# One PSUM tile of seven banks instead of two score tiles and three others, with a new written-out order, in an attention and Fourier-filter kernel

## The chip, the core and the metric

The kernel runs on one core of one Trainium2 chip. TensorE (PE in the profile) multiplies, VectorE (DVE) and ScalarE (ACT) read its results out of PSUM, GpSimd (POOL) works on SBUF, and SyncE (SP) issues most of the transfers. Inputs come from and the output goes to device memory. The metric is the device time of one execution in microseconds (us); the kernel before took 381.3 us as the median of three runs (380.2 to 381.46).

## What is computed

The input x has 2048 tokens of 448 features. One half of the result is self-attention with 16 heads of 28 features and a full softmax over all 2048 keys, then a projection with wo. The other half is a Fourier filter over the whole 2048x448 array. A gate per token mixes the two.

```
qkv = (x @ wqkv).reshape(B, S, 3, 16, 28) ...        # q, k, v per head
p   = softmax(q . k * 28**-0.5)                       # 16 heads, 2048 x 2048 each
a   = (p . v).reshape(B, S, 448) @ wo
b   = irfft2(rfft2(x) * (w_r + 1j * w_i))             # over tokens and features
g   = sigmoid((x * gate_w).sum(-1))
out = g * a + (1 - g) * b
```

## The kernel before

**Attention.** The heads lie in four groups g of four; a head is padded to 32 rows, so that the four heads of a group fill the 128 partitions. Queries are cut in four chunks c of 512. So there are 16 outputs n = (g, c). For each of them the kernel goes through 16 key tiles kt of 128 keys, and each key tile has four units, one per head s. The score of a unit is one matmul of a 32x128 tile of k against 512 queries; matmuls of different heads sit in different row tiles of the array and run side by side (a row pass). The result fills one PSUM bank of 128x512 numbers.

A unit then goes one of two ways. In 187 key tiles ("a") ScalarE takes the exponential of two banks at a time (line 1034, 374 times, 1024 numbers per partition) into `ring`, an SBUF buffer of 28 slots, and four matmuls in four column tiles multiply it with v into the bank `pvb` (a column pass). In the other 69 key tiles ("d", list `ND`) VectorE turns a score into the bits of a bf16 power of two by one add and clamp to uint16 (line 993, 276 times, one bank each); GpSimd makes three more phases of it by an integer add (line 1003, 207 times); and all four phases go through their own column pass into `pvb`. When an output n is complete, VectorE copies `pvb` out (`normalise`, line 1166 and, for the last one, 1137), takes reciprocals, and multiplies (lines 1178 and 1159).

**The rest.** The projections of q, k and v, the Fourier transforms as matmuls with constant matrices, the product with the filter weights, and the output (`out_tile` and `last_tile`, lines 1208 and 1229: eight column passes for each 128 tokens, four of the Fourier rows `X` against `Bd`, 224 columns wide, and four with wo, 448 wide) are called background. They are put between the scores.

**PSUM.** `alloc` (line 330) shares out the eight banks: `psA` and `psB` (lines 334 and 335), two banks each, hold scores for ScalarE alone and are used in turn; `pvb` is one bank; three banks `bgt` (line 337) serve everything else, the scores of the "d" tiles included. An operation that needs one of the three has an `Item`, whose bank number is set before it is emitted.

**The order.** The operations of the whole kernel are first collected by `Sched.op`. The order in which they are emitted, and so the order on each engine, is written out in `TABLE`, a compressed list of operation numbers with a list of bank numbers; `Sched.run` (line 275) goes through it, and a number from 60000 on emits a filler, a matmul whose result nobody reads (line 681, six passes). `pin` (line 302) holds every instruction at its place in its engine's order. Nothing is chosen at run time: an engine that reaches an instruction whose data or whose bank is not ready waits there, and everything behind it on that engine waits as well. The waits themselves are worked out by the framework per tile: two instructions that touch the same PSUM tile are ordered, also where they touch different banks of it.

Of the kernel before, what the change touches and what calls it, by code (L numbers as in the profile page):

```python
# [29 lines left out]
UNITS = 128.0  # L30
# [8 lines left out]
    "eNoN1mNjWEsUQNHxnMG5SW2ltm3bNtPUtm3btm3bto3UdvveX9hf1jakJbHEkXCCJDqJQWKSWCQ2iUPikngkPiEkAUlIEpHEJAkJI0lJMpKc"  # L39
    "UJKCZCApSU6SiniSmuQijHQlQAKiCScZSRoiSXaSlkQlitQk6Ugmkp7UILVINZKNZCG5SVUSheQhWUkOUodkJiVJKRKNlCa1SV5SloSQUFKO"  # L40
    "1Cf5SH5SgBQiBUkxUp6UIRVJYVKEFCXFySZSgWwmlUgJ0oq0JVvIVrKStCPbyHayiqwmVcgOsoZMJGtJZTKJTCZTyFSyjqwnG0g3YpVXG8l0"
    "MoPMJLOIU7PJHDKX7CTziCDzySy/gCwkcWk8Gp8uIovJDL+ELCUJaEK6jKDaRRLRnqQxWU5WkECFqMQ0Ck1Co9JoNDqNQcNoTBqLxqZx6G6y"
    "h+wl+0ioak6iqqfkGXlOXpCXJILcIQ3IfhJJ7pID5B55RV6TKOo+eUMekI7kIXlEHpNo6iCJrqaRGKouOUSS0mQ0pupEYqnkNAU9TJ6Qt2SD"
    "j63ekfckjvpA4qp4qhc5Qo6SlDS+akGOkan0I/lEptHPpAlJoBKq6fQLSaS+Qip6nCRWJ0hqmkR9gxk0TH0lp8hpkoau8WnpGXKWJFX1SG9y"
    "jpwnF8hMepEkU61JOnqJXCZXyFVyjSRX18kNcpOkULfIbZKeplRlaAaakZ4kmWhinoSnUj+hLE2t0qhYvByNzcvTXxCNz/XpVFpVgX6H6Dy9"
    "oqYiHUQyqIzqG0nGm5HvJAaPyX+Qn6Qp+UUyqT+QWf2DSjSLyqo6k+okDk/OK9OGpArtSDvRuDwhX+ezqc60C82uEvD1PhEP439IUp5D/SX/"
    "CKGUMrrac9qV5lSCSqqoprkU0Kw0G81Oc9DcKif9TXLR3NRQS/PQPCovzUdTcEfzKk/z05keaUDj83wqhBagmWlBWogWpkVofpWFhtJ4vCgt"
    "RtuTNqQ47U4LqIw8E+9BS9Ke1PJCyhhtHC+oCqv0vIjiJgMvTaUppoqqtLy4siYlr0p70RKqGi2pqtNSKh0vrVJzYXrTUlSZYaSMKkHT8Bq0"
    "Jk3FmSmrsvFyipi/UF5l5dn5SFpB5eGjaEU1mlZSeXkOPobWopVVB/IbqqiqKhcfS535AdVUTg6mNq2ucvMaqh7tQurTBjQfr0NrKm9qqc+u"
    "MC/DG9J4Bk1dWlsV4XVUDNOI1FUFeEJTkNdTCUwjmpnXV1l4WV6IJzHFeQlegefnFXkDFcs0VDFNXFOTN1KNVWNandfg8U0TVZQnMk1VMhOY"  # L50
    "YryZim1K8lo8jglXIaa5qsRb08o8mklpWqgIVY6X5m1oW9qOtlItVXnenjbjrVUqE86/uaimB2mjEpsmtK1KbkJNO1WVN6XNeQQPM9X4F9de"
    "NeFNeQeV0Xx3P9xP98t1VN1oJ1WX1+MZTDjtoprT7qSz+u0iaBTzx1XhLWhX1ZK2591UJlOKd1cduPQ9lPLpTHrTU/VSrWhtXoeDN9763iqN"
    "6aNa8+imr3I+tRlMve+n0po2vL8aQtE34o35ABX4gSqFSWoym0FqKB1GB6shqi3/6xrwf244JZ76+rwdH6oa8qKG+WGqI2/FC5jhqqDpxkeo"
    "fIb7Qkb4kWqU6sU78eKmO89jSpjRKovpzceoljyr6UvGqh68Jw/xXXkLXsaE+qG8GR2n8prxqjOP7xP4YTyhH8wnqES+iBnC4/i4PrGfqPrQ"
    "SWqyym860C58iipsipmpKokP81F9NN+HT1PZTHRf2cTw09UMNVP15aVNH5LT9KWzVAqf0s9Wa30qH9PH8rF9at+PpvFlzRy1kKb1i+hiOosu"
    "oXPVUprOD+fzVDkzgvfn5c18NYYvUHfoXXqPrqD36QO6ki5UI+gq+pA+oo/pE7qarqFP6SI1lq+l6+h6uoEO4BvpM7pYae/5JjqOL1HP6Qu6"
    "mb6kkXQ8f0WXqtd0C91Kt9FBdDtdpsbT5WoCXaFWquV0IK9kNvoddBwdSEuZQTypX6WS+Yl0El2tZvI1ajKdzquZmmatGs1n8XVqvZrEa5iS"
    "pqLZoPrxyXwG36jm8lF8Np9CJ/A5fCTfpPrTWmYi36yqmwF0Hp/Ct6gKpoqparapZXyrmk13qCW8tgk3c+g0nstsV03MPLpTNTUr+HKewyzl"
    "u1Qzs1vN5xFmj1rE1/LspoVZyTfyxXw+3ac6mTw+r9+rxpCFPJ9fx/P7TfyAmkv3qwK+oG9r2pmD6pA6rPbwOqa1mcqbm728kD+idvBMfifP"
    "7LP4oyqr38wHkGPqFF1AT9Mz9Cw9R7P54+o8vUCz+xz+Ir1EL9MTajW/Qrfwq3QVv0av0xv0pKprbtJTah9fw7uaBby/6WNu0dv0jFrPT6vc"  # L60
    "Zj9vY97QKL6zOad20rNqF91N99DzagPfS/fR/fQAPUgP0QtqFz9Md/Mj9Cg9Ri+q43QZPUFP8kuqgzlJT/GO5hzfzi+ro/wYv6KuqlZmG+9h"
    "eprz/Dg/wa+pLia9v64y+BvqMK9nuptDPLk/wluam+qWus/7mduqgq/oe5mG5gG/o7byC/wir+Qr+7uqij/IQ3goz+jbmwO8kbmnBphu5r6q"
    "6h+om7yaf6j6mt7mPb3C39K7fKCpbx6pW/yxOs3P8idqmhllnqqrfDi5xO/xZ2qcGW/e0RfquXrCL/OyfqIp55/ya3y0eakiVRPfwLxSTf0Y"
    "81rd5s38ZPNGhfs7/AV/q5r7l/ydivAzTDFf3JfwJX0p38K/V/PNB9WflPaRfJB5xT+qT2q2iefL+Bv8DL/OJ5np5rP6ogabIeQRf8af88J+"
    "gvmqvqnH/Av/yhubsaaIf8inmO/qh+JMsE/8p/qlPvOpRjLFNBtK3vJ3/D3/rf6omWaO+av+8n98sVloiP7AP/J/SorlZpYhYoihWgmm+5Hh"
    "huvXfK5ZYRaZN/w3L+qFpuIPlzqnz+V/8G+8oVda6wXmO8/th5lGfpmJKn5y0L+40UvMPPM/SMLqbn6p8drpaMIK1N39SpOE9fA9fS8PLLro"
    "7QO9yYSxpGyECdGhOoZIxvr47aaxj6qFiKKTMycOmW2Gieg6mtYiVHgRQ4OIIraY3SamiCVi6h1mp6nuY+lAxNYJxFGTUMTRIWK/SSJQ1PBx"
    "dZjYZ/aYeDq+TqDjiaEmvqjla/s6vq6v51eZ1SaRSCzq+7giqWjgy/uEerOZ7deYRHqUH+3H+LE+sR7nx/sJfq+ZQE6aOT6JDtNpxFbT0ifV"
    "yXRynVa08W19O9/exxEXTAff0Y80KXRKvc7U9J38QdPKf6Cp9Ef6iaYTqXUanVwcM+nFZ5pWp9OpRGyRXp8xJ8xh84WmFhl0Rl1I7DKFRV/f"
    "z6cQ030ykUmfNwdMZp1FZ9U5RUqRS3T2XXwGsdYcN9l0PnHKZNcD/EA/yGcU+cVgP8Tn0Dl1EXHEFBWnTSaRS2cVQ/1Zk1vHYHl0NnHOxGTD"  # L70
    "fD6dV180XX1mEYtlEbFZft3f3zIFdEEdh2UXf+h685fmEHlEIb3BFNYlxT9aStwx5UURTVgFQVleUVQ/N7lFaXHJFNNTfHE91d8zZcRDU0KX"
    "1DXEffPAlNI1RWldQBQU70w8VkaXFa19OXHbxGfFxHBfVidgI3xCVk1UFIlYdVFOV9Dl9RNTQnyjE/1I/9J8pxV1FVFJ/6A/aRU9yVfWTQVj"
# [12 lines left out]
    "U9q8dp8eT1aIjWKd2Kv36/2sgH3r3/n14r3fLg7oD/6gzmQz2t3ijz+kc9jDOredJI7ojz4G7hBbRRq7XETDbSI6bhEMOR7Vm8UecUwLlKgw"
    "nx1Ljuv8NgquFCf0IZHTHhbZ7Cl9Um8Sx8RpndXmscdFIXtR7BS7xBl9Vj9iUfGcLm0vifO6rP3kjwiNKfCCvqgT2fK2kt0vjopL+ry4IB6z"
    "z/4Je8qesefssn7BEtuXDDCSXdFX9QFR1Ra2X/xX/82H4EFxTV/XBr97iw5Pin3ih7+hf3qPr9hr9oa9Ze/Ye/aZfWE3dSgmQ8QPLMymwq/s"
    "G/vObukAf7Cf7Bf7zf6wU+Iju63/sn+McMoZT2I5F1zyT0zxIlbzO7qujYmx8J6+q88Kw+/rcyI2PtA17EN9QsTBuFjLPtJl7GPd1D7RT/UN"
    "cVqcERVtftwrilrgDWxSvCmSY3X7TN8R5ewL/VxfEdfEXVHBXhUvdU1b2UbqW+K6aGar2Nvitf4oXumH4q1OauvY+PhGV7PvdD0bD9/rR+KD"
    "fixei8b2nvgkGtrc+EYUt0/EU/FMfNT17XvxSafEB2Ic+azTYFr8opvYy+K5+CC+6m/6vhhMvuu34oX4od+JdFjSNrKpsbYNt7/Eb/FTJ8CE"  # L90
    "+FtPs790HpxrE+EfnR6jyb96tk2MSbC5/Sr+6RmWQE78IiiE4UL7Sqy0GXC6jS6L2T+CwSLL4a/4JiKsAAk/BJM/RQk7x5ZHBS9FC5sLNcy0"
    "30V4JMDn/yNHCiGVLGXzopTz7SxLZT400NpaqIwgIyIjIsMjPRhZCQugg4qYCQtiIQwAYZmdZzOiliHwTxTGIhgim2KoDIVGWAwzYxRwMgtm"
    "xbU2KkSDKHK5XWC9jA4r7BYbX8aEGBBVZsPVNjvmwApYFFHGlbGgLMaTCWRsiAPlcIndbAO5waaWcWGNjQexpZVxZBOMD4ttAiAyjayCVTEh"
    "xJAJ5SqbCBLJxJBcxpRLbRKohsUxDFLINrYEtrQlcb1tjEkhqayONTCWbGWTQSlMDutsMtkQN9pNNptMIrfagSQFpISUsjtml6lgnz1sU0Mq"
    "GY5poDQ2wywyTJbBbnjUHrFpoQdmlekgvcwkM8sDNj3klRlkBsgom2MEnrTpZCbYZlvgVZtPZoQskBlq4il7yGaFlphbtsI2WEK2xmyQHY7b"
    "WnjOlpR5ZCmZA3LCdlsbc8mxWAfrYmfMBfttaTkaz9vckAfyQj28aLtgfbxh88t8kB8aYGKZVra1PfGgzSkLQEFZEE7YArKY7IqFoJDMIQvL"
# [1374 lines left out]
```

## Time and profile before

| | us |
|---|---|
| runs, median (lowest, highest) | 381.3 (380.2, 381.46) |
| span of the profiled execution | 379.2 |
| TensorE busy | 371.3 (98%) |
| VectorE busy | 339.1 (89%) |
| ScalarE busy | 351.1 (93%) |
| GpSimd busy | 234.4 (62%) |
| first and last exponential, start | 12.74 and 364.96 |

The profiled execution has a span of 379.2 us from its first to its last instruction; the timed runs were 1.0 to 2.26 us longer, the median 2.1. A row of the timeline gives the start, the duration, the engine, the line and operation, output and inputs by the program's names, and how many instructions the row holds. TensorE's matmuls are pipelined: several run side by side, and the end of one overlaps the start of the next, so that the time a pass costs is read from the distance between starts and not from the duration in the row. 32\*128 in a row is the tile of the array: 32 rows by 128 columns is a row pass, 128\*32 a column pass. TensorE's clock was granted in full throughout.

### The profile page before, as it was taken

Reading aid. Unit: us, or ns where it says so; the run is one execution under the profiler, and the core shown is the slowest. Engines: PE = TensorE matmul, PEld = TensorE weight load, DVE = VectorE, ACT = ScalarE, POOL = GpSimd, SP = SyncE. Lnnn points to the kernel's source line nnn. Section 1 sums busy time; section 2 is a strip of 40 time slices with the busy share of each in tenths; the row PEclk is TensorE's granted clock in tenths of the full one; section 3 lists DMA queues with packets and bytes.
Section 4 is the critical chain, followed back from the end, with each engine's and each line's share of the span. In section 5 each row is a group of like instructions: output and inputs, shape, how many; then the busy total and the mean of one; then the engine's idle time right before and its main releaser. Section 6 shows DMA issues by size and latency. Waiting matters only on the chain.

```text
span 379.2 us, 12643 instructions
## 1 busy us (share of the span) xinstructions
PE 371.3 (98%) x5117; PEld 142.4 (38%) x5117; DVE 339.1 (89%) x665; ACT 351.1 (93%) x389; POOL 234.4 (62%) x264
## 2 busy tenths in 40 slices
PE   8999999999999999999999999999999999999996
PEld 6634223342433333234333434233333323433564
DVE  1768899999999999999999999999999999988744
ACT  2799999999999999999999999999999999999841
POOL 4446465866778866565553565778597778483510
PEclk9999999999999999999999999999999999999999
DMA  6511101010210112211322212223222122222132
GB/s 145 157 34 44 29 18 36 4 36 2 41 52 22 44 41 54 55 38 30 68 60 93 69 40 49 57 61 70 45 64 74 30 69 72 86 64 72 35 103 75
DMA packets 31158, 21.23 MB, mean 56 GB/s; under 512 B 16260, under 2 KB 29052, under 8 KB 31100
## 3 DMA queue, kind: packets, MB, share of 16 engines
q1 hardware_dynamic: 29708, 19.96, 20.7%
q8 instruction: 40, 0.66, 0.7%
q10 hardware_dynamic: 1392, 0.46, 0.5%
q14 instruction: 18, 0.15, 0.1%
HBM read 14.51 MB, written 1.96 MB: 43 GB/s over the span
## 4 chain that ended last, share of the span: by engine, by line
PE 55%; ACT 31%; issue 6%; DVE 4%; DMA 2%; POOL 1%; SPq 0%; DVEq 0%; ACTq 0%; POOLq 0%
ACT ring L1034 31%; PE bg L432 24%; PE pvb L432 17%; PE psA L432 7%; PE psB L432 6%; DVE pd L993 2%; PE bg L435 1%; DMA CS<-cCS 1%; DVE X L1419 1%; POOL pd L1003 1%; DMA Wg<-in_B_w_i_dram 0%; DVE X L1298 0%; DVE q L1178 0%; DVE t L1362 0%; DVE wpq L1224 0%
## 5 line engine op out<-in xcount | busy, mean ns | idle before, releaser
L1003 POOL INT64_ADD pd<-pd x207 | 211.9, 1038 | 96.7 <-DVE pd L993 27.4
L1034 ACT ACTIVATE ring<-psA 128x1024 bf16<-128x1024 f32 x187 | 201.7, 1078 | 4.7 <-PE psA L432 3.2
L1034 ACT ACTIVATE ring<-psB 128x1024 bf16<-128x1024 f32 x187 | 201.7, 1079 | 2.6 <-PE psA L432 1.4
L993 DVE TENSOR_SCALAR pd<-bg 128x512 uint16<-128x512 f32 x276 | 180.9, 681 | 8.5 <-PE bg L432 3.5
L432 PE MATMUL pvb<-pd,vd 128*32 128x512 bf16 x1104 | 96.9, 384 | 0.1
L432 PE MATMUL bg<-q,k 32*128 32x512 bf16 x276 | 96.3, 383 | 0.2
L432 PEld LDWEIGHTS <-k 32*128 32x128 bf16 x1024 | 40.1, 91 | 122.4 <-issue 117.7
L432 PE MATMUL psB<-q,k 32*128 32x512 bf16 x374 | 73.2, 383 | 1.3 <-ACT ring L1034 0.7
L432 PE MATMUL psA<-q,k 32*128 32x512 bf16 x374 | 72.8, 383 | 0.5 <-ACT ring L1034 0.2
L432 PE MATMUL pvb<-ring,vw 128*32 128x512 bf16 x748 | 67.9, 384 | 0.0
L432 PEld LDWEIGHTS <-vd 128*32 128x32 bf16 x1104 | 25.3, 94 | 35.5 <-issue 31.1
L432 PEld LDWEIGHTS <-vw 128*32 128x32 bf16 x748 | 17.5, 94 | 22.7 <-issue 20.5
L432 PEld LDWEIGHTS <-xT 128*128 128x128 bf16 (+5 forms) x512 | 20.3, 97 | 10.7 <-issue 9.7
L432 PE MATMUL bg<-xT,wpq 128*32 128x512 bf16 (+3 forms) x244 | 21.2, 383 | 0.1
L1362 DVE TENSOR_TENSOR t<-bg,Wg 128x450 bf16<-128x450 f32 x32 | 18.8, 614 | 0.6 <-DMA Wg<-in_B_w_i_dram 0.4
L432 PE MATMUL bg<-xT,wpk 128*32 128x512 bf16 (+2 forms) x240 | 18.9, 383 | 0.0
L432 PE MATMUL bg<-wvr,xT 128*128 128x112 bf16 (+2 forms) x192 | 13.7, 213 | 0.0
L1178 DVE TENSOR_TENSOR q<-pvs,Rb 128x512 bf16<-128x512 f32 x15 | 10.9, 729 | 2.6 <-DMA Rb<-rsc 2.6
L1298 DVE TENSOR_TENSOR X<-bg,oc 128x226 bf16<-128x226 f32 (+1 forms) x32 | 12.3, 386 | 0.5
L432 PEld LDWEIGHTS <-CS 128*32 128x32 bf16 x384 | 9.0, 95 | 9.9 <-issue 5.6
L432 PE MATMUL bg<-xtok,CS 128*32 128x225 bf16 (+1 forms) x192 | 11.2, 294 | 0.7 <-DMA CS<-cCS 0.7
L742 DVE TENSOR_SCALAR k<-bg 128x512 bf16<-128x512 f32 x15 | 10.3, 685 | 1.3 <-PE bg L432 1.1
(117 smaller groups left out, 315.4 us busy)
## 6 DMA issues: line engine op xcount, KB each, us to landing
Rb<-rsc SPq DMA_DIRECT2D x60, 64.0 KB
CS<-cCS SPq DMA_DIRECT2D x16, 192.0 KB
V<-xtok SPq DMA_DIRECT2D x16, 113.0 KB
Wg<-in_B_w_i_dram SPq DMA_DIRECT2D x64, 28.1 KB
xtok<-Ab SPq DMA_DIRECT2D x16, 112.5 KB
xtok<-in_A_x_dram SPq DMA_DIRECT2D x3, 448.0 KB
Wg<-in_B_w_r_dram SPq DMA_DIRECT2D x32, 28.1 KB
out_dram<-wpq SPq DMA_DIRECT2D x6, 112.0 KB
```

The lines of the kernel that those rows point to most:

```text
L432: self.pin(self.nc.tensor.matmul(out, lhsT=lhsT, rhs=rhs, start=start, stop=stop, **kw))
L435: self.pin(self.nc.tensor.transpose(out=out, in_=in_, identity=self.c("ident")[0:n, 0:n]))
L742: self.pin(nc.vector.tensor_scalar(out=dst, in0=self.bgi(it), scalar1=SQ, scalar2=None, op0=ALU.mult))
L993: self.pin(nc.vector.tensor_scalar(out=ys[:, s, :].bitcast(U16), in0=self.bgi(it), scalar1=127 * UNITS, scalar2=0.0, op0=ALU.add, op1=ALU. ...
L1003: self.pin(nc.gpsimd.int64_add(out=fl(pds), in0=fl(ys), in1=PHASE[f] * 0x0001000100010001))
L1034: self.pin(nc.scalar.activation(out=self.ring[:, u0:u0 + len(st), :], in_=slot[:, 0:len(st), :], func=ACT.Exp, scale=LN2 / UNITS))
L1178: e = self.dve(dv(512), lambda: self.pin(nc.vector.tensor_tensor(out=dst, in0=pvs[:], in1=self.Rb[:], op=ALU.mult)), ds, kk, lk=True)
L1298: self.pin(nc.vector.tensor_tensor(out=free_dims(self.X1[:, t, :], [[F, 2], [-1 if dif else 1, n]], (F - 1) * dif), in0=free_dims(self.bgi ...
L1362: self.pin(nc.vector.tensor_tensor(out=out[:], in0=self.bgi(it)[:, 0:F2].rearrange("p (a f) -> p a f", a=2), in1=free_dims(Wg[:], [[F, 2], ...
L1419: self.pin(nc.vector.tensor_tensor(out=free_dims(self.zt[0:FN], [[128, 4], [1, 128]], 512 * t), in0=self.bgi(it)[0:FN, :].rearrange("p (a ...
```

## The change

`psA`, `psB` and the three banks `bgt` become one tile `ps` of seven banks; `pvb` stays. Every score unit is now an operation of its own with a bank of its own out of the seven, and so are the transposes and projections at the start and the last output tiles, which used `psA` and `psB`. An exponential reads two neighbouring banks, whichever pair they are. As all seven banks are one tile, `pin` tells the framework for each instruction which banks it uses, and that it does not depend on instructions with other banks; what an operation names as its own inputs is kept. In 12 of the 69 "d" tiles two of the four clamps are put together as one instruction over two neighbouring banks (`PARTS`), which leaves 264 clamps. Due times, which were no longer used for the order, are taken out. `TABLE` now has four lists: 4001 operation numbers, 1199 banks, the widths of the exponentials (374, all two banks) and the parts of the 69 "d" tiles. The order is another one throughout, and it has no fillers.

```diff
 TABLE = (
-    "eNoN1mNjWEsUQNHxnMG5SW2ltm3bNtPUtm3btm3bto3UdvveX9hf1jakJbHEkXCCJDqJQWKSWCQ2iUPikngk
+    "eNoNltMSIDoWAMMTJ2Pbtm3btm3btm3btm3btnFn9w/6oaurFTKoJ9KoK2qKKqGOqBlyyKOGqBtqiyxCCCOC
...
+    def need(self):
+        return [p for d in self.op_now.deps for p in d.made]
...
+    PARTS = (((0,), (1,), (2,), (3,)), ((0, 1), (2, 3)), ((0, 2), (1, 3)), ((0, 3), (1, 2)),
...
     def pin(self, ins):
...
+        if self.sc.used:
+            used = frozenset(self.sc.used)
+            keep = [p for p, u in self.sc.need() if not used & u]
+            if ins.ins.engine in self.before:
+                keep.append(self.before[ins.ins.engine])
+            for other in self.bank_sets:
+                if not used & other:
+                    self.tc.declare_no_dep(ins.ins, group="bank" + repr(sorted(other)), reason="other banks",
+                                           keep=[k for k in keep if k.name in self.bank_sets[other]])
+            self.bank_sets.setdefault(used, set()).add(ins.ins.name)
+            self.tc.add_to_no_dep_group("bank" + repr(sorted(used)), ins.ins)
...
-        self.psA = ps.tile([P, 2, 512], F32, name="psA")
-        self.psB = ps.tile([P, 2, 512], F32, name="psB")
+        self.ps = ps.tile([P, 7, 512], F32, name="ps")
         self.pv = ps.tile([P, 512], F32, name="pvb")
-        self.bgt = [ps.tile([P, 512], F32, name=f"bg{i}") for i in range(3)]
...
     def bgi(self, item, dt=F32):
-        t = self.bgt[item.bank][:]
+        t = self.ps[:, item.bank, :]
+        self.sc.used.add(item.bank)
...
+            for part in self.PARTS[sc.parts[di]]:
...
+                    self.pin(nc.vector.tensor_scalar(
+                        out=free_dims(ys[:], [[512 * e, w], [1, 512]], 512 * part[0]).bitcast(U16),
+                        in0=self.ps[:, bs[0]:bs[0] + w, :],
+                        scalar1=127 * UNITS, scalar2=0.0, op0=ALU.add, op1=ALU.max))
...
-            slot = self.psA if i % 2 == 0 else self.psB
-            deps = [exps[i - 2]] if i >= 2 else []
+            deps, ms = [], []
...
+                it = uit[n, kt, s] = Item()
...
+                m = sc.op("PE", 0.22, fm, self.kev[g, kt // 4] + self.qev[g, c], 0.0, 0.0, "row", it, name="score")
...
+                self.pin(nc.scalar.activation(out=self.ring[:, u0:u0 + len(st), :],
+                                              in_=self.ps[:, bs[0]:bs[0] + len(st), :],
+                                              func=ACT.Exp, scale=LN2 / UNITS))
...
-        it = Item() if i > 1 else None
-        bank = lambda: (self.psA[:, 0, :] if i == 0 else self.psB[:, 0, :] if i == 1 else self.bgi(it))[:, 0:D]
+        it = Item()
+        bank = lambda: self.bgi(it)[:, 0:D]
```

Three places show how instructions move. The first is TensorE in the middle of the attention, at a row pass with scores for both ways. In the rows of before, `psB` and `bg` are scores of `q` and `k`, and the engine named in brackets is the one whose reading of the bank the matmul waits for.

```order
L432 MATMUL psB<-q_85,k_89 128x512 [waits Activation_49]
L432 LDWEIGHTS k_89
L432 MATMUL psB<-q_85,k_89 128x512
L432 LDWEIGHTS k_89
L432 MATMUL bg_64<-q_85,k_89 128x512 [waits DVE_49]
```

```order
L464 MATMUL ps<-q_81,k_85 128x512 [waits Activation_49]
L464 LDWEIGHTS k_85
L464 MATMUL ps<-q_81,k_85 128x512 [waits DVE_49]
L464 LDWEIGHTS k_85
L464 MATMUL ps<-q_81,k_85 128x512 [waits Activation_49]
L464 LDWEIGHTS k_85
L464 MATMUL ps<-q_81,k_85 128x512
L464 LDWEIGHTS k_85
L464 MATMUL ps<-q_81,k_85 128x512 [waits DVE_49]
```

Before, the two banks of a pair for ScalarE became free together, by one earlier exponential, and only a score for VectorE waited for VectorE. Now a pair may be put together from banks that different engines read last.

The second place is TensorE at the last scores of the program, with the output passes `Bd,X` around them.

```order
L432 MATMUL bg_66<-Bd,X_131 32x224
L432 LDWEIGHTS k_89
L432 MATMUL psB<-q_87,k_89 128x512 [waits Activation_49]
L432 LDWEIGHTS k_89
L432 MATMUL psB<-q_87,k_89 128x512
L432 LDWEIGHTS k_89
L432 MATMUL psA<-q_87,k_89 128x512
L432 LDWEIGHTS k_89
L432 MATMUL psA<-q_87,k_89 128x512
L432 LDWEIGHTS X_131
```

```order
L464 MATMUL ps<-Bd,X_127 32x224
L464 LDWEIGHTS k_85
L464 MATMUL ps<-q_83,k_85 128x512 [waits Activation_49]
L464 LDWEIGHTS k_85
L464 MATMUL ps<-q_83,k_85 128x512
L464 LDWEIGHTS k_85
L464 MATMUL ps<-q_83,k_85 128x512 [waits DVE_49]
L464 LDWEIGHTS k_85
L464 MATMUL ps<-q_83,k_85 128x512
L464 LDWEIGHTS X_127
```

The last four scores are one row pass in both. Behind them TensorE has 264 matmuls left before and 320 now: 14 output passes, eight of 224 and six of 448 columns, four matmuls each, have moved from ahead of the last scores to behind them.

The third place is VectorE at the first "d" tile, where `pd` is what a clamp writes.

```order
L993 TENSOR_SCALAR pd_115<-bg_64 128x512 [waits PE_49]
L888 TENSOR_SCALAR vd_116<-vt 128x20x29 [waits DVE_49,Pool_49]
L903 TENSOR_SCALAR ge<-ge 128x16 [waits Activation_49]
L993 TENSOR_SCALAR pd_115<-bg_66 128x512 [waits PE_49]
L888 TENSOR_SCALAR vd_116<-vt 128x20x29
```

```order
L1025 TENSOR_SCALAR pd_107<-ps 128x512 [waits PE_49]
L1025 TENSOR_SCALAR pd_111<-ps 128x512 [waits PE_49]
L914 TENSOR_SCALAR vd_112<-vt 128x20x29 [waits DVE_49,Pool_49]
L1025 TENSOR_SCALAR pd_111<-ps 128x1024 [waits PE_49,Activation_49]
L768 TENSOR_SCALAR k_85<-ps 128x512 [waits PE_49]
```

Here one clamp of 1024 numbers per partition stands for two of 512.

More of the change, by code (lines that the diff above doesn't have):

```diff
@@ L44 @@
[L44 to L48, printed above, removed]
@@ L557, in prologue @@
                            (warm,), K0 + i * .01, dur=0.175, acq=None if i else hw, free=hw if i == 19 else None)
[L559 to L560 removed]
+        hs = [None, Item(), Item(), Item()]
+        homes = [lambda: self.pv[:]] + [lambda h=h: self.bgi(h) for h in hs[1:]]
         trs, self.xev = [], {}
@@ L584, in prologue @@
             b1 = (lambda i1=i1: self.bgi(i1)) if wi else (lambda: self.pv[:])
-            b2 = (self.psB if wi else self.psA)[:, 0, :]
+            i2 = Item()
+            b2 = lambda i2=i2: self.bgi(i2)
             first = {}
@@ L1104, in attention @@
             if o.name == "score":
-                for u in self.steps[o.step]:
-                    kr[self.groups[u[0]][0]].append(o)
+                kr[self.groups[o.n[0]][0]].append(o)
         for m in self.dunit_ops:
```

307 lines of the change are left out of this document (164 added, 143 removed).

## The prediction

> **What bounds the kernel now.** I read the busy shares and the chain of waits first, and then the busy time of each engine by stretches of the span.
>
> ```profile
> span 379.2 us, 12643 instructions
> ...
> PE 371.3 (98%) x5117; PEld 142.4 (38%) x5117; DVE 339.1 (89%) x665; ACT 351.1 (93%) x389; POOL 234.4 (62%) x264
> ...
> PE 55%; ACT 31%; issue 6%; DVE 4%; DMA 2%; POOL 1%; SPq 0%; DVEq 0%; ACTq 0%; POOLq 0%
> ```
>
> ```profile
> 60.00:150.00 90.00, 89.17 (x1251) 31.25 (x1251) 87.55 (x175) 89.96 (x100) 65.03 (x67) 1.00 0.13 33
> 150.00:210.00 60.00, 60.00 (x857) 22.60 (x855) 58.51 (x116) 57.35 (x65) 31.46 (x33) 1.00 0.21 55
> 210.00:345.00 135.00, 132.74 (x1734) 46.40 (x1731) 129.78 (x262) 134.69 (x147) 95.92 (x96) 1.00 0.25 61
> 345.00:366.00 21.00, 21.00 (x400) 10.19 (x400) 13.44 (x22) 17.84 (x19) 9.23 (x9) 1.00 0.27 77
> ```
>
> The columns behind the length are PE, its weight loads, DVE, ACT and POOL. Three engines are nearly full at once. From 60 to 150 ACT is busy all the time (89.96 of 90) and from 210 to 345 almost (134.69 of 135); from 150 to 210 and from 345 on PE is, and ACT has holes (57.35 of 60, 17.84 of 21). DVE stands at 97% from 60 to 345 (87.55 + 58.51 + 129.78 = 275.84 of 285). So the lead changes by stretches, and what a change is worth depends on where it falls. Next I looked at how ACT's exponentials follow each other, and what they wait for.
>
> ```profile
> 12.74 1.02 ACT L1034 ACTIVATE ring<-psA 128x1024 bf16<-128x1024 f32 x1 [0.31 <-PE psB L432]
> ...
> 103.26 1.10 ACT L1034 ACTIVATE ring<-psB 128x1024 bf16<-128x1024 f32 x1
> ...
> 104.16 1.11 ACT L1034 ACTIVATE ring<-psA 128x1024 bf16<-128x1024 f32 x1
> ...
> 364.96 1.02 ACT L1034 ACTIVATE ring<-psB 128x1024 bf16<-128x1024 f32 x1
> ```
>
> ```profile
> ACT ring L1034 <- PE psA L432: 4.5, 8, 0.8
> ...
> ACT ring L1034 <- PE psB L432: 2.5, 6, 0.6
> ```
>
> Where nothing holds them, exponentials start 0.904 apart (104.16 - 103.26 = 0.90; by the trace's further digits 0.904). 373 such steps are 337.3, while first and last start 352.2 apart: 14.9 us of ACT's time go elsewhere, 7.0 of them (4.5 + 2.5, in 14 waits) named as waits for scores. The other 7.9 have no named releaser and are 0.02 for each step.
>
> **The change, priced.** PE's passes are priced from the distance between starts, where nothing else stands between.
>
> ```profile
> 102.74 0.39 PE L432 MATMUL psB<-q,k 32*128 32x512 bf16 x2
> 102.75 0.39 PE L432 MATMUL bg<-q,k 32*128 32x512 bf16 x1
> ...
> 103.07 0.61 PE L432 MATMUL pvb<-pd,vd 128*32 128x512 bf16 x8
> ...
> 103.61 0.39 PE L432 MATMUL psA<-q,k 32*128 32x512 bf16 x2
> ```
>
> ```profile
> 350.72 0.39 PE L432 MATMUL psA<-q,k 32*128 32x512 bf16 x2
> ...
> 351.04 0.40 PE L432 MATMUL pvb<-pd,vd 128*32 128x512 bf16 x4
> ...
> 352.37 0.39 PE L432 MATMUL psA<-q,k 32*128 32x512 bf16 x2
> 352.38 0.39 PE L432 MATMUL psB<-q,k 32*128 32x512 bf16 x2
> ...
> 352.69 0.39 PE L432 MATMUL bg<-wpq,q 128*32 128x448 bf16 x4
> ```
>
> ```profile
> 354.13 0.38 PE L432 MATMUL bg<-wpk,q 128*32 128x448 bf16 x4
> ...
> 354.33 0.38 PE L432 MATMUL bg<-wpq,q 128*32 128x448 bf16 x4
> ...
> 359.29 0.37 PE L432 MATMUL bg<-Bd,X 113*32 113x224 bf16 x8
> ...
> 359.48 0.37 PE L432 MATMUL bg<-wpq,q 128*32 128x448 bf16 x4
> ```
>
> A column pass 448 wide takes 0.20 (354.13 to 354.33), 224 wide 0.095 (two in 0.19 from 359.29), and by width 0.22 at 512. Two of 512 and the change of array tiling behind them take 0.54 (103.07 to 103.61), so a change of tiling costs 0.10. A row pass with the change behind it takes 0.32 with two units (350.72 to 351.04), with three (102.74 to 103.07) and with four (352.37 to 352.69): the pass is 0.22 however full it is. The instructions of both orders, counted from first to last score, differ in four things:
>
> - Tiling changes: 713 before, 691 now. 22 x 0.10 = -2.2.
> - Row passes of scores: 382 before, 374 now, since full passes of four become more frequent (32 to 64). 8 x 0.22 = -1.8.
> - The six fillers, 128 to 256 wide: by width -0.5.
> - 14 output passes that now stand behind the last score: 8 x 0.095 + 6 x 0.20 = -2.0.
>
> That is -6.5 between first and last score. Behind the last score the same 14 passes come back, +2.0, if PE is full there:
>
> ```profile
> 366.00:379.20 13.20, 9.67 (x244) 7.02 (x236) 6.80 (x12) 1.55 (x2) 0.00 (x0) 0.99 0.22 72
> ```
>
> ```profile
> 375.28 0.39 PE L432 MATMUL bg<-wpk,q 128*32 128x448 bf16 x4
> ...
> 375.72 0.71 DVE L1224 TENSOR_SCALAR wpq<-bg,glog 128x448 bf16<-128x448 f32 x1 [0.44 <-PE bg L432]
> 376.46 0.33 SPq L407 DMA_DIRECT2D out_dram<-wpq  x1
> ```
>
> It is: the 9.67 busy reach from 366 to 375.67, where the last matmul ends; the last eviction and transfer, 3.5, stay. So moving the 14 passes is worth nothing by itself, and PE's sum falls by 4.5: 379.2 - 4.5 = 374.7 if every part of it is on the path.
>
> The same from ACT's side. I added up each order's passes to the scores of each pair and took off 0.904 per pair. Where this balance climbs, PE is the later one and ACT waits. Before it climbs by 1.0 up to pair 45, by 4.0 from 135 to 225 and by 3.0 from 330 to the end, 8.0 in all, which agrees with the 7.0 of named waits. Now it climbs by 0.1, 2.8 and 0.3, 3.2 in all: -4.8 between the first and the last exponential, and with the +2.0 behind it -2.8. There is a further gain in this account: before, ACT's two pairs of banks let PE be at most two pairs ahead; seven banks can hold a third, 0.90 more of ACT's work, which eats into the climb of 2.8 and at the front of the others. I take up to -1.2 for it, down to 0 where VectorE's scores hold the banks. So this account gives -2.8 to -4.0, PE's -4.5. I choose PE's, since PE has the longer share of the chain (55% against 31%), and keep the other as the upper end.
>
> **The pair clamps.**
>
> ```profile
> 348.27 1.89 DVE L993 TENSOR_SCALAR pd<-bg 128x512 uint16<-128x512 f32 x3
> ```
>
> ```profile
> L993 DVE TENSOR_SCALAR pd<-bg 128x512 uint16<-128x512 f32 x276 | 180.9, 681 | 8.5 <-PE bg L432 3.5
> ...
> L1362 DVE TENSOR_TENSOR t<-bg,Wg 128x450 bf16<-128x450 f32 x32 | 18.8, 614 | 0.6 <-DMA Wg<-in_B_w_i_dram 0.4
> ```
>
> One clamp takes 0.681 and three in a row 1.89, so a further one costs 0.60, two 1.28. No clamp of 1024 is in the trace. The nearest row for the slope is another operation: 62 elements more make 614 ns into 681, 1.08 ns each, so 512 more make 1.234. A pair saves 0.05, and 12 save 0.6 on DVE; the ends are 0 and 0.13 each (all of the fixed part), 0 to 1.6. I take it as hidden at PE (0 on the sum): PE leads in the stretches that the sum shortens. What it costs: PE has to fill two neighbouring banks before the clamp starts.
>
> **The transposes and projections at the start, waits per bank, units as own operations.** They give the same instructions (PE 8.3 before the first score in both); the sum carries nothing for them. What the waits themselves can cost is the third rival.
>
> The profiled execution is 2.1 below the median. 374.7 + 2.1 = **376.8**.
>
> [...]
>
> [...]
>
> **The rivals.** *ACT never waits* (chance 0.14). With up to three pairs in hand all 7.0 of named waits go and part of the 7.9 as well. Its exponentials would run from 12.74 to 350.0 (+337.3) if all of the 14.9 went and to 357.9 if only the named did; 14.2 lie behind the last start now and 2.0 more then: 366.2 to 374.1, middle 370, as a run 372. For it: 60 to 150, where ACT is 89.96 of 90 busy. Against it: the balance still climbs by 3.2, and DVE at 97%.
>
> *The saving comes back* (0.13). DVE is nearly full from 60 to 345, and in this stretch it has the same clamps, products and copies to do. If it keeps the pace there, only its own 0.6 is saved in the stretch, PE waits for banks that DVE has not read, and the 14 passes were only moved, 2.0 out and 2.0 in: 379.2 - 0.6 = 378.6, as a run 380.7. Against it: the named waits of ACT for PE lie where PE, not DVE, is full.
>
> *Score pairs wait for VectorE's banks* (slower, 0.11). Before, 2 of the 748 score units for ACT went into a bank that DVE had read last; now 146 do, as the built program's waits show. PE keeps its order, so such a wait holds all that is behind it, first of all the column passes into `pvb` and the scores for DVE. DVE's queue moves in steps of 0.60 (the clamps), while ACT has about 0.90 in hand. A reader that is two places late (1.20) makes ACT lose 0.3. From 15 such events (4.5) the gain is gone; 25 give 7.5: 374.7 + 7.5 = 382.2, as a run 384.3. For it: DVE at 97% is late as a rule, not by chance. Against it: those units sit in an order in which a DVE read may lie far ahead of them, and PE's waits for DVE fall in number (453 to 431).
>
> *The banks are not told apart* (0.02). If the waits were still by tile, every pair would wait for the readers of all seven banks; 374 times 0.3 would be over 100 us. The waits in the built program are all on a reader of the same bank.
>
> **How the numbers follow.** The forecast has 0.60. Its own range is 374.5 to 379.2: below by the third pair (1.2) and the pair clamps (0.6) and half a microsecond of scatter, above by ACT's account (-2.8, so 378.5) and 0.7 of scatter, as the three runs lie 0.6 around their middle. About 0.3%, 1.15 us, is what a measurement of this kernel can tell from no change: faster is below 380.15, slower above 382.45. Forecast (0.58 of its 0.60) and first rival (0.14), with a small part of the second (0.03), make faster 0.75; the rest of the second and 0.02 of the forecast 0.12 same; third and fourth 0.13 slower. The range goes from 371.5 (half of the first rival) to 381.6 (the second with scatter); left out are 0.07 below and 0.13 above.
>
> **What would show it.** Step by step: row passes of scores still 0.32 from start to start with the change behind them, and PE's distance from first to last score shorter by 4 to 7 us; the named waits of exponentials for PE near 3 instead of 7.0, most of them about a third to a half of the way; the distance from the last score to the last matmul longer by 2.0 than 11.7 (363.55 to 375.28); a clamp of 1024 at 1.23. Waits of PE scores for DVE in the list of waits, over 5 us in all, would show the third rival; DVE at over 98% from 60 to 345 with PE's idle time grown, the second; first to last exponential under 345, the first. Wrong would be the forecast where PE's sum falls and its busy share falls with it, so that the end stands still.

## The result, and the profile after

The changed kernel takes 405.0 us as the median of five runs (402.8 to 410.7) against 381.1 before: 1.0626 times as long, with an interval of 1.0567 to 1.0686. The ratios here and below leave out the executions in a slower state of the chip, here the one of 410.7. The forecast of 376.8 missed the sign and the range.

The page of the changed kernel's profile: the span, the busy shares, the granted clock of TensorE in 40 slices, and the chain that ended last.

```profile
span 406.9 us, 12439 instructions
...
PE 382.8 (94%) x5093; PEld 143.6 (35%) x5093; DVE 360.4 (89%) x653; ACT 356.7 (88%) x389; POOL 240.6 (59%) x264
...
PEclk9999999999999999999999996968698999999999
...
PE 47%; DVE 23%; ACT 6%; issue 4%; POOL 2%; DMA 2%; SPq 1%; POOLq 0%; DVEq 0%; ACTq 0%
```

Two things are new. VectorE is busy 21.3 us longer (360.4 against 339.1) although it has twelve instructions fewer, and its part of the chain has grown from 4% to 23%, while ScalarE's fell from 31% to 6%. And TensorE's clock, granted in full before, drops in some slices from 240 us on (0.966 in the mean of this execution). The waits that the forecast watched went the other way: the exponentials wait for scores 44 times and 26.6 us (7.0 before, about 3 forecast), and TensorE waits for clamps, which it never did for long before.

```profile
ACT ring L1075 <- PE ps L464: 26.6, 44, 2.2
...
PE ps L464 <- DVE pd L1025: 8.7, 11, 1.6
```

Where VectorE's 21.3 us come from is read from its groups, line by line with the mean duration. First before, then the change:

```profile
L1178 DVE TENSOR_TENSOR q<-pvs,Rb 128x512 bf16<-128x512 f32 x15 | 10.9, 729 | 2.6 <-DMA Rb<-rsc 2.6
...
L888 DVE TENSOR_SCALAR vd<-vt 128x580 bf16<-128x580 f32 x16 | 7.2, 470 | 0.1
L747 DVE TENSOR_TENSOR sq<-q 128x512 bf16<-128x512 bf16 x15 | 6.3, 433 | 0.0
L747 DVE TENSOR_TENSOR sq<-k 128x512 bf16<-128x512 bf16 x15 | 6.2, 429 | 0.1
...
L1367 DVE TENSOR_TENSOR Z<-t 128x225 bf16<-128x225 bf16 x16 | 4.6, 300 | 0.0
...
L1369 DVE TENSOR_TENSOR Z<-t 128x225 bf16<-128x225 bf16 x16 | 4.2, 270 | 0.0
...
L1169 DVE RECIPROCAL rr<-rs 128x16 f32<-128x16 f32 x15 | 3.6, 241 | 0.0
```

```profile
L1025 DVE TENSOR_SCALAR pd<-ps 128x512 uint16<-128x512 f32 x252 | 165.6, 682 | 12.3 <-PE ps L464 8.8 <-ACT ring L1075 1.0 <-POOL pd L1039 0.8
L1217 DVE TENSOR_TENSOR q<-pvs,Rb 128x512 bf16<-128x512 f32 x15 | 15.9, 1063 | 0.4 <-DMA Rb<-rsc 0.4
...
L1025 DVE TENSOR_SCALAR pd<-ps 128x1024 uint16<-128x1024 f32 x12 | 14.6, 1218 | 0.8 <-PE ps L464 0.7
...
L914 DVE TENSOR_SCALAR vd<-vt 128x580 bf16<-128x580 f32 x16 | 10.6, 702 | 0.1
...
L773 DVE TENSOR_TENSOR sq<-q 128x512 bf16<-128x512 bf16 x15 | 9.9, 673 | 0.0
...
L773 DVE TENSOR_TENSOR sq<-k 128x512 bf16<-128x512 bf16 x15 | 8.5, 574 | 0.1
L1408 DVE TENSOR_TENSOR Z<-t 128x225 bf16<-128x225 bf16 x16 | 7.9, 496 | 0.0
L1406 DVE TENSOR_TENSOR Z<-t 128x225 bf16<-128x225 bf16 x16 | 7.8, 488 | 0.0
...
L1208 DVE RECIPROCAL rr<-rs 128x16 f32<-128x16 f32 x15 | 3.6, 243 | 0.0
```

The clamps, which read PSUM, take 682 ns as before (681). Six groups, of which all inputs lie in SBUF, take longer: the multiplication of a finished output by its reciprocals 1063 ns against 729, the values for the "d" tiles 702 against 470, the squares of q 673 against 433 and of k 574 against 429, the differences of the filter (L1367 before, L1406 now) 488 against 300 and its sums (L1369 and L1408) 496 against 270. Together that is 21.2 of the 21.3 us. The reciprocals, 16 numbers per partition out of SBUF, do not take longer (243 against 241), although 7 of the 15 lie beside one of GpSimd's adds. One place in the timeline shows what happens (start, duration, engine and line):

```profile
44.94 2.05 POOL L1039 INT64_ADD pd<-pd  x2
...
45.53 1.73 DVE L773 TENSOR_TENSOR sq<-q 128x512 bf16<-128x512 bf16 x1
47.18 1.28 DVE L1025 TENSOR_SCALAR pd<-ps 128x512 uint16<-128x512 f32 x2
...
47.92 0.37 PE L464 MATMUL ps<-q,k 32*128 32x512 bf16 x1 [1.01 <-DVE pd L1025]
...
48.32 1.02 ACT L1075 ACTIVATE ring<-ps 128x1024 bf16<-128x1024 f32 x1 [1.17 <-PE ps L464]
```

GpSimd has two adds from 44.94 to 46.99. VectorE's square starts at 45.53 and ends at 47.26, after both, though it needs 0.43 alone. The clamp behind it is late, TensorE waits 1.01 for the bank, and the exponential behind that 1.17. Over the whole trace 48 such VectorE operations overlap a GpSimd add, for 42 us together; before there are 13, for 4 us. Counted in the two programs, 57 GpSimd instructions are held behind such an operation before and 34 now: `pin` makes the GpSimd instruction that is emitted next after such an operation wait for it, and the new order has fewer places where the operation comes first.

The falls of the clock follow waits of TensorE. By stretches of 5 us (length, then busy time of PE, its weight loads, DVE, ACT and POOL, then the clock):

```profile
240.00:245.00 5.00, 4.73 (x60) 2.23 (x57) 4.89 (x10) 4.71 (x7) 4.30 (x4) 1.00 0.38 83
245.00:250.00 5.00, 3.16 (x22) 0.57 (x22) 5.00 (x8) 2.37 (x4) 2.63 (x3) 0.67 0.20 51
250.00:255.00 5.00, 5.00 (x47) 1.16 (x43) 3.33 (x7) 3.91 (x5) 3.09 (x3) 0.65 0.17 31
255.00:260.00 5.00, 4.91 (x54) 1.50 (x53) 4.95 (x8) 5.00 (x6) 3.35 (x4) 1.00 0.27 70
```

```profile
243.16 4.47 POOL L1039 INT64_ADD pd<-pd  x4
...
244.22 4.10 DVE L914 TENSOR_SCALAR vd<-vt 128x580 bf16<-128x580 f32 x4
...
246.79 0.62 PE L464 MATMUL pvb<-pd,vd 128*32 128x512 bf16 x4 [1.83 <-DVE vd L914]
```

Four operations of 0.45 take 4.10 beside four adds, TensorE waits 1.83, and from 246.66 to 253.48 its clock is at half.

### The profile page after: what moved, and what is told of

Read it like the earlier page. It is cut to its first block, busy times and chain, and to the rows that moved or that the text cites. A ratio compares the mean times of both kernels' runs of the same rounds, so it can differ in the third digit from the quotient of the medians.

```text
span 406.9 us, 12439 instructions
## 1 busy us (share of the span) xinstructions
PE 382.8 (94%) x5093; PEld 143.6 (35%) x5093; DVE 360.4 (89%) x653; ACT 356.7 (88%) x389; POOL 240.6 (59%) x264
## 4 chain that ended last, share of the span: by engine, by line
PE 47%; DVE 23%; ACT 6%; issue 4%; POOL 2%; DMA 2%; SPq 1%; POOLq 0%; DVEq 0%; ACTq 0%
PE ps L464 29%; PE pvb L464 18%; DVE pd L1025 9%; ACT ring L1075 6%; POOL pd L1039 2%; DVE t L1401 2%; DVE sq L773 2%; DVE q L1217 1%; DVE vd L914 1%; DVE Z L1408 1%; DVE Ab L1354 1%; DVE Z L1406 1%; DVE X L1337 1%; DVE xtok L1432 1%; SPq L439 1%
## 5 line engine op out<-in xcount | busy, mean ns | idle before, releaser
L1075 ACT ACTIVATE ring<-ps 128x1024 bf16<-128x1024 f32 x374 | 351.5, 1050 | 27.6 <-PE ps L464 26.6
L1025 DVE TENSOR_SCALAR pd<-ps 128x512 uint16<-128x512 f32 (+1 forms) x264 | 179.4, 706 | 13.0 <-PE ps L464 9.5
L464 PE MATMUL ps<-q,k 32*128 32x512 bf16 x1024 | 152.7, 394 | 10.4 <-DVE pd L1025 6.7
L464 PE MATMUL ps<-xT,wpq 128*32 128x512 bf16 (+4 forms) x248 | 19.8, 382 | 0.9 <-POOL wpq L542 0.9
L464 PE MATMUL ps<-xT,wpk 128*32 128x512 bf16 (+3 forms) x244 | 18.9, 383 | 0.5 <-DVE t L1401 0.4
L1401 DVE TENSOR_TENSOR t<-ps,Wg 128x450 bf16<-128x450 f32 x32 | 19.0, 616 | 0.3
L1217 DVE TENSOR_TENSOR q<-pvs,Rb 128x512 bf16<-128x512 f32 x15 | 15.9, 1063 | 0.4 <-DMA Rb<-rsc 0.4
L464 PE MATMUL ps<-wvr,xT 128*128 128x112 bf16 (+1 forms) x192 | 13.0, 213 | 0.7 <-DVE vt L905 0.7
L464 PE MATMUL ps<-Bd,xT 128*32 128x226 bf16 (+2 forms) x256 | 11.9, 264 | 1.1 <-DVE pd L1025 0.7
L1337 DVE TENSOR_TENSOR X<-ps,oc 128x226 bf16<-128x226 f32 (+1 forms) x32 | 12.3, 387 | 0.6
L1432 DVE TENSOR_TENSOR xtok<-ps,oc 128x226 bf16<-128x226 f32 x32 | 11.5, 383 | 0.3
```

The source lines that it names most:

```text
L464: self.pin(self.nc.tensor.matmul(out, lhsT=lhsT, rhs=rhs, start=start, stop=stop, **kw))
L1025: self.pin(nc.vector.tensor_scalar(out=free_dims(ys[:], [[512 * e, w], [1, 512]], 512 * part[0]).bitcast(U16), in0=self.ps[:, bs[0]:bs[0] ...
L1075: self.pin(nc.scalar.activation(out=self.ring[:, u0:u0 + len(st), :], in_=self.ps[:, bs[0]:bs[0] + len(st), :], func=ACT.Exp, scale=LN2 / ...
L1217: e = self.dve(dv(512), lambda: self.pin(nc.vector.tensor_tensor(out=dst, in0=pvs[:], in1=self.Rb[:], op=ALU.mult)), ds, kk, lk=True)
L1337: self.pin(nc.vector.tensor_tensor(out=free_dims(self.X1[:, t, :], [[F, 2], [-1 if dif else 1, n]], (F - 1) * dif), in0=free_dims(self.bgi ...
L1401: self.pin(nc.vector.tensor_tensor(out=out[:], in0=self.bgi(it)[:, 0:F2].rearrange("p (a f) -> p a f", a=2), in1=free_dims(Wg[:], [[F, 2], ...
```

## The experiments

Two theories were set against each other. Theory C: these six groups of VectorE operations, with inputs in SBUF, and GpSimd's adds exclude each other; the new order makes them meet, and VectorE's delay is the loss. Theory B is the third rival of the prediction: score units sit in banks that VectorE reads, and wait for it.

**Structure alone.** The order of before, emitted through the new structure: `TABLE` holds the old operation numbers translated, banks 0, 1 and 2, 3 for the two score tiles, 4 to 6 for the three others, and single clamps.

```diff
+        self.ps = ps.tile([P, 7, 512], F32, name="ps")
+        (TABLE: the order and the banks of before, all parts single)
```

> The order of before in the structure of the change: seven banks in one tile, waits declared per bank, every score unit an operation of its own, no pair clamps; the banks stand for the old tiles (0,1 and 2,3 for the two score tiles, 4 to 6 for the three others). If the new structure costs nothing by itself and the loss lies in the new order and its banks: 380 to 382.5. If the waits per bank or the single units cost something: over 384.

380.95 us, 0.9994 times before (0.9982 to 1.0006). One tile of seven banks, waits declared per bank and units as operations of their own cost nothing; the loss lies in the order, with its banks, or in the pair clamps.

**The holds taken out of the kernel before.**

```diff
-        if ins.ins.engine == mybir.EngineType.Pool and self.port is not None:
+        if ins.ins.engine == mybir.EngineType.Pool and False:
```

> The kernel before, without the extra dependency that holds a GpSimd instruction until the VectorE operation on two SBUF inputs ahead of it has ended; nothing else is changed. In the profile of before 12 of 83 such operations overlap an add, 4 us in all, in the changed kernel 47, 41 us. Theory C: overlaps come up here too, VectorE's busy time grows by 8 or more, and the time by 4 to 25 us. Theory B: 380 to 382, since no bank and no order changes. If VectorE's busy time grows and the time does not, contention alone is not what costs.

405.2 us, 1.0621 times (1.0589 to 1.0654). Old banks, old order on every engine, no pair clamp, and nearly the same loss as the change. VectorE's busy time is 358.1:

```profile
PE 380.9 (95%) x5117; PEld 142.3 (35%) x5117; DVE 358.1 (89%) x665; ACT 354.9 (88%) x389; POOL 239.1 (60%) x264
```

```profile
PE bg L432 <- DVE pd L993: 6.8, 9, 1.7
```

TensorE's waits for clamps come up here too (6.8 us), so those of the changed kernel need no new banks. This speaks against theory B.

**A fill in place of the adds, in the changed kernel.**

```diff
-    self.pin(nc.gpsimd.int64_add(out=fl(pds), in0=fl(ys), in1=PHASE[f] * 0x0001000100010001))
+    m = nc.gpsimd.memset(pds[:].rearrange("p a b -> p (a b)")[:, 0:1116], 1.0)
+    (m waits for the same clamps as the add did)
```

> The changed kernel, with GpSimd's integer adds (after the first use of each of the nine buffers) replaced by a fill of 1116 of the 2048 numbers: about the same 1.04 us on GpSimd, behind the same clamps, but it reads no SBUF. The phases that it leaves out are then wrong, everything else runs as before. In the changed kernel VectorE is busy 360.4 us against 339.1 before, all of it in operations on SBUF inputs that overlap an add (multiplication of the outputs 1063 ns against 729, squares 673 and 574 against 433 and 429, differences and sums of the filter 488 and 496 against 270 and 300, values for the d tiles 702 against 470). Theory C (these operations wait for GpSimd's adds at SBUF, and VectorE's delay is the loss): VectorE's busy time falls to 335-345, the waits of TensorE for the clamps fall from 8.7 to under 3, the granted clock is back at 0.99 or more, and the time is 375 to 384. Theory B (the rival of the prediction: scores sit in banks that VectorE reads, whatever GpSimd does): time 398 or more, TensorE still waits 7 or more for clamps. If only the values for the d tiles still contend (one SBUF input), about 385.

390.7 us (1.0242 times before, 1.0197 to 1.0288), 14.3 less than the change; the expectation of 375 to 384 was too low. GpSimd is as long at work (1.033 us a fill), but reads nothing:

```profile
L914 DVE TENSOR_SCALAR vd<-vt 128x580 bf16<-128x580 f32 x16 | 11.0, 730 | 0.1
L1227 DVE TENSOR_TENSOR q<-pvs,Rb 128x512 bf16<-128x512 f32 x15 | 10.2, 682 | 1.4 <-DMA Rb<-rsc 1.4
```

The multiplication, with two inputs in SBUF, is back at 682 ns, also in the 12 of 15 cases that lie beside a fill, and the filter's differences are at 273, its sums at 270. The values for the "d" tiles, with one input in SBUF, are still at 730: the fill holds them too, four of them in a row from 238.69 on take 4.20 us beside four fills, and TensorE runs at half clock from 243.59 to 250.42 behind them. VectorE's 342.5 us and TensorE's waits for clamps (1.7) are as expected, the clock of 0.985 to 0.996 and the time are not; the case in which only these values still contend had been put at about 385. So more than half of the loss goes without GpSimd being any shorter or earlier: what counts is which of its instructions meets which of VectorE's.

For operations with two inputs both halves are measured on the multiplication: 1063 ns in the change, where GpSimd's adds read SBUF, and 682 here, where its fills only write. In the change VectorE also lost twice in a row (1.73 for a square behind two adds).

**Short adds, in both kernels.**

```diff
-    self.pin(nc.gpsimd.int64_add(out=fl(pds), in0=fl(ys), in1=PHASE[f] * 0x0001000100010001))
+    w = 64 if id(pds) in self.pdnew else 512
+    self.pin(nc.gpsimd.int64_add(out=fl(pds)[:, 0:w], in0=fl(ys)[:, 0:w], in1=PHASE[f] * 0x0001000100010001))
```

> The changed kernel, with GpSimd's integer adds cut to an eighth of their elements after the first use of each buffer (the rest of the phases is left out): GpSimd neither holds SBUF nor is late. Theory C: 374 to 381, VectorE busy 335 to 342, clock 0.99 or more; close to the run with the fill, or below it by what GpSimd's lateness costs. Theory B: 398 or more. If it is well below the run with the fill (over 5 us), then GpSimd's own lateness, and not SBUF, is the larger part.

> The kernel before with GpSimd's adds cut to an eighth after the first use of each buffer (the rest of the phases is left out): the reference for the changed kernel with the same cut, which took 383.9. Before loses only 4 us to overlaps, of which VectorE has little to spare: 379 to 381.3 expected. If it comes out near 379, the new order is by 5 slower with no contention at all; at 376 or less, GpSimd costs both orders about the same.

383.9 us for the change (1.0076 times before, 1.0049 to 1.0102) and 380.96 for before. So 21 of the change's 24 us go with the adds, and 3.0 stay. Before gains nothing from short adds (0.9999, 0.9988 to 1.001): its order had already kept them out of VectorE's way.

```profile
PE ps L464 <- DVE pd L1025: 1.4, 3, 1.0
```

The change with short adds still has its new banks, and yet TensorE's waits for clamps fall from 8.7 to 1.4. That speaks against theory B in the changed kernel itself. It lies 6.8 below the run with the fill, which by the sign named (over 5) would make GpSimd's lateness the larger part. The traces have other reasons: with the fill VectorE is busy 3.3 longer (342.5 against 339.2), and TensorE is at half clock for 10.2 us between head and tail, with short adds never. How much of the 6.8 is lateness, if any, was not separated. The first theory covers the bulk; the 3.0 are the part of the forecast that remains to be explained, below.

**Holds put back into the change.** Each engine's order stays, but at 27 places the VectorE operation is emitted ahead of the add.

```diff
+        (TABLE: 27 SBUF operations of VectorE emitted ahead of the GpSimd add they would meet)
```

> The changed kernel with its order on every engine kept, but written out so that at 27 places a VectorE operation on SBUF inputs is emitted ahead of the GpSimd add that would overlap it, which makes the add wait for it. Before has 57 such holds, the changed kernel 34. Theory C (adds and these VectorE operations exclude each other at SBUF): VectorE's busy time falls from 360 to 345-353 and the time to 388-398; not the whole loss, since at the other places holding the add would make the passes that need it late. If the holds are not what matters: 403 or more.

395.4 us (1.0390 times before, 1.0334 to 1.0446), 9.6 less than the change, VectorE busy 348.3. Both lie inside what was expected, and by design it is not all: a held add makes the column passes late that read it. Already here TensorE waits 2.5 us in five places for a phase that GpSimd adds.

**Pairs taken apart.**

```diff
+        (TABLE: all 69 parts single, the same order and banks)
```

> The changed kernel with the 12 pair clamps taken apart into 24 single ones, everything else (order, banks) the same. The pairs save 0.06 us each (1.218 against 1.28), 0.7 in all: if they are only that, 404 to 407, and the waits of TensorE for clamps stay. If the pairs are a reason for the loss (two banks have to be full before one clamp starts): under 401.

409.5 us (1.0739 times before, 1.0715 to 1.0763), above the expected 404 to 407. The pairs are no cause of the loss. Single clamps cost 4.5 more than the change, of which VectorE's 1.4 (361.8 against 360.4) is one part; how much of the rest is the clock, 0.974 to 0.978 here and 0.966 to 0.987 in the change, was not separated.

**VectorE late at one place, and in eight small pieces.** In the kernel before, clamps are repeated: one of them eight times, or eight of them once each.

```diff
-                def f1(s=s, it=it, ys=ys):
+                def f1(s=s, it=it, ys=ys, rep=8 if (di, s) == (50, 3) else 0):
+                    for _ in range(1 + rep):
```

> The kernel before with one clamp, the last of the 51st d tile, done nine times instead of once (the result is the same): VectorE is late by 8 x 0.60 = 4.8 us at one place, nothing else changes. If VectorE has no room: 385.5 to 387. If in addition TensorE's granted clock is halved after it has waited (in the profiles so far all seven waits of 1.8 us or more are followed by one to three stretches of 3.41 us at half): one or two such stretches, 1.7 to 3.4 more, 387.5 to 390, and a mean clock of 0.98 to 0.99. If VectorE's delay is absorbed: 381 to 383.

> The kernel before with the last clamp of every eighth d tile done twice (eight places): the same 4.8 us more on VectorE as in the run with eight at one place, which cost 8.9, but in pieces of 0.60. If VectorE sets the pace: 385 to 386. If pieces of 0.6 are absorbed by what lies ready: 381 to 383. If the half clock comes by the sum of waits and not by a long one: over 388.

Eight at one place cost 8.9 us (389.8; 1.0236, 1.0215 to 1.0257), eight in pieces 4.8 (385.6 against 380.85; 1.0129, 1.0108 to 1.0150), for the same 4.8 us of VectorE. The pieces are not absorbed at all: at those eight places VectorE sets the pace. At one place TensorE waits 5.7 us, and then runs at half clock for 10.2:

```profile
283.77 0.75 PE L432 MATMUL bg<-xtok,CS 128*32 128x450 bf16 x8 [5.69 <-DVE pd L994]
```

```profile
277.00:284.00 7.00, 1.31 (x15) 0.52 (x16) 6.73 (x11) 2.46 (x3) 2.08 (x3) 0.86 0.17 36
284.00:291.00 7.00, 7.00 (x60) 1.49 (x52) 4.62 (x8) 4.10 (x4) 4.67 (x5) 0.50 0.05 8
```

**New orders with these exclusions priced.** The last three runs have the structure of the change, the banks of before and single clamps, and each a new order, found by small moves from that of before.

```diff
+        (TABLE: a new order; banks of before; all parts single)
```

> The seven-bank structure with the banks of before and single clamps, in another order: from the order of before, instructions were moved by small steps on their engines, as long as a replay of the program became shorter in which a GpSimd instruction and a VectorE operation on SBUF inputs exclude each other (the replay has durations and distances from the profile of before; it gives 382.3 for before, 407.7 for the changed kernel, 394.0 for the one with 27 holds, which measured 394.1). The replay gives 374.9 here, 7.4 less than before. Theory C, that the cost of an order lies in what is late on VectorE: 372 to 378, VectorE busy at most 340, no stretch at half clock. If the replay only fits its own prices: 380 or more, as for the changed kernel.

> A second order found in the same way from another start of the search; the replay gives 375.7. Expected 372.5 to 379 by the same theory. If one of the two is faster and one is not, the replay is not to be relied on.

> As the first of the two new orders (seven-bank structure, banks of before, single clamps, searched from the order of before with exclusions of VectorE and GpSimd priced), but the replay now also charges SyncE 0.38 to 0.67 for the issue of each transfer, as the trace has it, and 1.0 to 2.0 until it lands; the first two orders had 0.1 there, and lost 5.2 and more in one wait for the constants of the Fourier step. The replay gives 374.5 against 386.0 for before by the same prices. If exclusions and transfers are what those orders got wrong: 368 to 378, longest wait of TensorE under 1.5, no stretch at half clock. If something else is missing: 381 or more.

399.1, 403.3 and 385.2 us (1.0481, 1.0582 and 1.0107 times before, the last with 1.0088 to 1.0126), all slower than before and outside what was expected. In the first VectorE is as wanted (339.7), but TensorE waits 5.2 for one transfer that stands in SyncE's queue behind seven others, and half clock follows (0.980 in the mean). The second waits 7.1 near its start for GpSimd's `wpk`, and 5.1 in two waits for the same constants. The first one's wait:

```profile
PE ps L458 <- DMA CS<-cCS: 5.2, 1, 5.2
```

The issue of those transfers had been priced at 0.1 each where the trace has 0.3 to 0.7. With that mended the third has no such wait, a full clock (1.000), VectorE at 338.1, and the named waits of its exponentials are 8.1, about the 7.0 of before:

```profile
PE 371.9 (97%) x5093; PEld 141.3 (37%) x5093; DVE 338.1 (88%) x665; ACT 351.2 (92%) x389; POOL 234.1 (61%) x264
```

```profile
PE ps L458 <- POOL zero L527: 3.2, 1, 3.2
...
ACT ring L1069 <- PE ps L458: 8.1, 16, 0.9
```

Its tenth exponential starts 2.7 us later than before and its last 2.4 later: it loses at the start, where TensorE waits 3.2 for a buffer to be cleared (1.1 before), and 1.3 behind the last exponential, and in the whole middle it gains 0.3. The 7.4 and 11.5 us that the replays had given were not there to be had, or not by these prices. No version beat the kernel before.

## Why the prediction was wrong

**The step that failed** is the cost of VectorE's part: "in this stretch it has the same clamps, products and copies to do", and 0.6 less for the pairs. The sum of the forecast has no term for VectorE at all: the pair clamps stand in it with 0, and everything else was taken as unchanged. The counts were right, but they were priced with the durations of before. The duration of six of its groups is no property of the operation alone: it depends on which GpSimd add stands beside it, and that is set by the order of two engines against each other. The two rows of the multiplication (729 and 1063) show the term that was missing, 21.3 us on VectorE. It could have been seen ahead of the run: in the order, by the count of GpSimd instructions that wait behind such an operation (57 to 34), and in the trace of before, where the multiplication's mean of 729 ns is made of thirteen rows of 674 to 697 and of two, of 974 and 1081, that lie beside an add.

**The choice of TensorE as the engine that rules** was wrong too. I set the pair clamps to nothing as "hidden at PE". VectorE's lateness reached the end 1 for 1 in the run with eight pieces. The row that I had quoted, VectorE 97% busy from 60 to 345, was the right one, and I gave it 0.13 as a rival with a gain of 0.6 instead of asking what VectorE's operations would cost in the new order.

**TensorE's 4.5** does not appear even where most exclusions are gone. With short adds in both, the change is 3.0 slower, and VectorE's remaining exclusions can be some 2 of it (busy 339.2 against 337.2). From first to last exponential it takes 354.3 against 353.0, where -4.8 was forecast from ScalarE's account; the exponentials wait 7.6 for scores in both, where the account had 3.2 against 8.0. In the last new order the distance is 353.7, and before 352.2: in four runs of three orders with different sums on TensorE it has stayed within 2.1. What went against the -4.8 in the change is seen in three places of the run with short adds: TensorE waits 1.3 for an input at the start (transposes moved ahead of their data), the adds of the first use of each buffer, which are still whole, cost 1.3 around 46 (two exponentials start 2.23 apart), and a multiplication waits 1.3 for its transfer at 147, which the order had put too early. That these three are the whole of it is not shown.

**The tail** was right: +2.0 forecast for the 14 passes moved behind the last score; from the last score to the last matmul the change takes 13.7 against 11.8, and behind the last exponential 2.1 more (16.36 against 14.23).

**The pair clamp** was right in size (1.234 forecast, 1.218 measured), wrong in worth, as said.

**The third rival** had the sign, with 0.11, and its chain is the one in the trace (VectorE late, TensorE waits for a bank, exponential late). What was named to show it, over 5 us of waits of TensorE for VectorE, came true as well (8.7 for clamps alone). But its mechanism, scores in VectorE's banks, is not what makes it: the old banks lose as much (405.2) when the holds are taken out, and the new banks lose little (383.9) when the adds are short. Its price, 0.3 for a reader two places late, was too low where a single operation is 1 us late (26.6 us in 44 waits are 0.6 each), and had no half clock in it.

**The fourth rival** drops out with the first experiment: the structure is free. **The semaphores** are not settled by it: that program has 955 matmuls that release a reader, as before, and not the 1041 of the change. The kernel before with short adds has 995 and took no longer (0.9999, 0.9988 to 1.001); whether some of the 3.0 left in the change belongs to its semaphores is not shown.

## What to carry to other kernels

Where VectorE and GpSimd run side by side, price a new order by pairs: for each VectorE operation with SBUF inputs, what GpSimd does at that moment; a count of the instructions held back, before and after, is a cheap first look. Find out which engine passes its delay on 1 for 1 (repeat a harmless instruction in eight places) before a saving on another engine is put into a sum. A sum of work on the engine with the longest chain says nothing about transfers and buffers that an order now asks for earlier.

## What the runs showed of the hardware

- In the change VectorE operations with two SBUF inputs and GpSimd adds held each other up: a square of 0.43 became 1.73 behind two adds, and an add issued 0.07 behind a multiplication took 1.51 (at 216.3) where alone it takes 1.04. In the run with the fill, which only writes, squares (0.42), the multiplication (0.68) and the filter's differences and sums (0.27) keep their time in 39 overlaps; the values with one f32 input do not (0.91 to 1.37 against 0.45). The small reciprocals, with one input, keep 0.24 beside either (243 ns in the mean of both runs).
- In the change's trace TensorE's clock goes to half for 6.83, 10.24, 6.83 and 3.41 us (from 246.66, 267.14, 284.20 and 308.10) and is full for 13.65, 6.83 and 17.07 between them: whole multiples of 3.41 us, on one grid. Over the fourteen traces, and without the head and the tail of the kernel, stretches of 3.41 us at full clock in which no matmul was in flight for 1.25 us or more were followed by half clock in all 17 cases; of those with 0.75 to 1.2, in 4 of 22; of those with 0.5 to 0.75, in none of 29. In the change the stretches ahead of its four falls had 1.70, 1.81, 1.33 and 0.75 us without a matmul, so well under half of a stretch idle was enough.
- The changed kernel's executions lie as far apart as their clocks: 402.8 and 403.3 us at 0.987, 405.0 at 0.979, 408.7 at 0.966. Drawn on to a full clock that is about 399.5, an estimate: some 5 of the 24 us would be the clock, if nothing else sets these executions apart. As half clock follows TensorE's waits, most of which are for VectorE here, these 5 are rather a part of the loss than a second cause.
